# Scores of two heads in 64-row tiles of TensorE, instead of one head doubled over 128 rows

## The chip, the cores and the metric

The kernel runs on one core of a Trainium2 chip. The metric is the device time of one execution in microseconds (us); lower is better. The core has five engines that run side by side and wait for each other by semaphores: TensorE (PE in the profile; its weight loads are PEld), VectorE (DVE), ScalarE (ACT), GpSimd (POOL) and SyncE (SP), which here issues the DMAs.

## What is computed

An attention with a narrow window and block summaries is followed by a mixture of four dense experts, all in float32. The part that the change touches is the scores:

```python
B, H, S, D = 4, 8, 768, 64        # q, k, v; block, window = 32, 16
k_sum = k.reshape(B, H, nb, block, D).max(axis=3)
scores_l = scale * np.matmul(q, k.transpose(0, 1, 3, 2))       # only |i - j| < 16 counts
scores_s = scale * np.einsum('bhsd,bhnd->bhsn', q, k_sum) + np.log(block)
a = softmax(concat(where(mask_l, scores_l, -1e9), scores_s))
x = matmul(a, concat(v, v_sum))                                 # 3072 tokens of 512
# experts: out += p[:, e] * (relu(x @ w1[e]) @ w2[e]),  w1: 512x1024, w2: 1024x512, e = 0..3
```

## The kernel before

**Pieces.** Attention is cut into 64 pieces `n`: batch `b = n // 16`, a block `i` of 96 queries, and a group `g` of four heads. A piece of 96 queries sees 128 keys (its window) and the 24 block maxima of k, so its scores are 96 x 152 for each head. The first 8 pieces run by a path of their own (`first_tokens`, `piece`), with plain float32 products; the other 56 go through `load_piece`, `stage_a`, `scores`, `probs`, `transposed`, `values` and `to_x`.

**A piece before.** `load_piece` (line 519) issues two DMAs: `kr`, 128 partitions x 4 heads x 128 keys from `kD`, which holds k twice (once in partitions 0 to 63, once in 64 to 127), and `qv`, four heads of q (doubled over the partitions in the same way) beside v. `stage_a` (528) copies the block maxima behind the keys on POOL, and splits k into a high part (rounded to the fp32r type, ACT) and a low part (POOL), two heads at a time; q is rounded on ACT, and POOL overwrites partitions 64 to 127 of it by the low part. A head has 64 features, so one matmul with 128 rows multiplies q's high part (rows 0 to 63) and q's low part (rows 64 to 127) with k's high part at once, and a second one with k's low part: two products per head, four heads, eight matmuls `psc` per piece. `scores` (561) is called twice per piece, `half` 0 and 1, with two heads each; each half has one PSUM bank, the tile `psc`. VectorE then reads the bank, adds the mask and finds the maxima (`ms`, `nb`), and ScalarE takes the exponentials. Further on, `values` (625) issues the matmuls `px`: 12 of them per piece (16 in the first batch), each with 64 output columns, two at a time side by side in the array.

**The banks.** PSUM has three pools: `ps_mm` (4 banks), `ps_sc` (2 banks, tag `sc`) and `ps_av` (2 banks). The tag `sc` has a second user: when two token blocks are worked as a pair (`first`, line 1420, and `second_sevens`, 1325), the accumulator with key `a` of each unit, `pha` or `poa` in the profile, also takes an `sc` bank. In `first`, a unit is seven products of six matmuls in the order a, d, b, a, b, c, b; bank `a` is held from the first product until the fourth has been read.

**The experts.** `plan` gives six stages: token block 0 with experts 0 and 1, block 1 with experts 1 and 0, both with experts 2 and 3 (fp32r matmuls `ph`, `po`), then three pairs of token blocks (16-bit float matmuls `pha` to `phd`, `po`, then `poa` to `pod`). Between their units `advance` (1501) calls the attention steps whose key is due: `scores` half 0 at k, half 1 at k + 0.3, `values` at k + 2.0 (k + 1.5 for n below 16), so that the values of piece n and half 0 of piece n + 2 fall on the same place.

**The order.** Nothing is issued where it is called. Each call records a `Step`, and `order_of` (162) puts all of them into one order: it plays the program with its own durations (`PE`, `ACT`, ... from line 109), gives the buffers of a tag to its tiles in the order in which they are first used, and lets TensorE take, of the matmuls whose operands and whose bank are there, the one that comes first in the written order. A tile whose bank is still held isn't there yet, and TensorE goes on with other matmuls. On the chip each engine then follows its list in order and waits where it must.

**Block maxima of k.** `setup_k` (453) loads k by pairs of heads (`kch`), VectorE takes the maxima into `ksr`, and `spread_k` (445) doubles them into `ks` with four small DMAs; for batch 0 `first_tokens` calls `spread_k` (line 965).

Of the kernel before, what the change touches and what calls it, by code (L numbers as in the profile page):

```python
# [10 lines left out]
F32 = mybir.dt.float32  # L11
F32R = mybir.dt.float32r
# [3 lines left out]
ALU = mybir.AluOpType  # L16
AX = mybir.AxisListType

P = 128
B, H, S, D = 4, 8, 768, 64  # L20
E, DM, DF = 4, 512, 1024
BLK, WIN = 32, 16
NB = S // BLK
QB = 96
KW = 128
KA = KW + NB
NQ = S // QB
G = 4
# [5 lines left out]
SCALE = 1.0 / math.sqrt(D)  # L34
# [25 lines left out]
def _win0(i):  # L60
    return min(max(QB * i - WIN, 0), S - KW)
# [7 lines left out]
def columns(ap):  # L69
    return math.prod(n for _, n in ap.ap[1:])  # L70
# [15 lines left out]
class Step:  # L86
# [22 lines left out]
    def PE(self, op, kw):  # L109
        n, w = self.moved(), self.read[0]  # L110
        if op == "transpose":
            return 95.0, 260.0
        if w.dtype == F32:
            return 65.0 + 1.75 * n, 230.0 + 1.75 * n
        if columns(w) == D:
            return 22.0 + 0.18 * n, 215.0 + 0.25 * n
        t = max(70.0, 0.453 * n) + 15.0 * (n < 200) if w.dtype == F32R else max(45.0, 0.4235 * n)
        return t, t + 165.0

    def ACT(self, op, kw):  # L120
# [167 lines left out]
def attn_moe(ctx: ExitStack, tc: tile.TileContext, qvL, qv0, v0L, kD, kT, vT, w1L, w2L, dpL, cst, out):  # L288
# [3 lines left out]
    class Engine:  # L292
# [5 lines left out]
        def __getattr__(self, name):  # L298
# [3 lines left out]
            return issue  # L302

    V, A, PL, PE, SP = (
        Engine(e, k)
        for e, k in ((nc.vector, "DVE"), (nc.scalar, "ACT"), (nc.gpsimd, "POOL"), (nc.tensor, "PE"), (nc.sync, "SP"))
    )
# [12 lines left out]
    def pool(name, bufs=1, **kw):  # L320
        return Pool(name, bufs, **kw)
# [3 lines left out]
    def spare_x(n):  # L325

        return n % 2 == 1 and n < XFREE

    sb = pool("sb")
    ps_mm = pool("ps_mm", 4, space=bass.MemoryType.PSUM)  # L330
    ps_sc = pool("ps_sc", 2, space=bass.MemoryType.PSUM)
# [98 lines left out]
    ksum = {}  # L430
# [5 lines left out]
    def load_chunk(b, hp, ch, src):  # L436
        SP.dma_start(ch, src[b, 2 * hp : 2 * hp + 2].rearrange("h d s -> (h d) s"))

    def block_stats(ch, dst, hp, op):
        V.tensor_reduce(dst[:, hp, :], ch.rearrange("p (n k) -> p n k", k=BLK), axis=AX.X, op=op)  # L440

    def chunk(name):
        return sb.tile([P, S], F32, name=name, tag="chunk", bufs=CHUNKS)

    def spread_k(b, ksr):
        ks = sb.tile([P, H, NB], F32, name=f"ks{b}", tag="ks", bufs=2)
        ks_v = ks.rearrange("p (a j) n -> p j a n", j=2)
        for half in range(2):
            for j in range(2):
                SP.dma_start(ks_v[half * D : (half + 1) * D, j], ksr[j * D : (j + 1) * D])  # L450
        ksum[b] = ks

    def setup_k(b):
        ksr = sb.tile([P, G, NB], F32, name=f"ksr{b}", tag="ksr")
        for hp in range(H // 2):
            ch = chunk(f"kch{b}_{hp}")
            load_chunk(b, hp, ch, kT)
            block_stats(ch, ksr, hp, ALU.max)
        spread_k(b, ksr)

    def setup_v(b):
        vsr = sb.tile([P, G, NB], F32, name=f"vsr{b}", tag="vsr")
# [55 lines left out]

    def load_piece(n):
        b, i, g = n // 16, (n // 2) % NQ, n % 2  # L520
        h0, w0 = g * G, _win0(i)
        kr = sb.tile([P, G, KA], F32, name=f"kr{n}", tag="kr", bufs=2)
        qv = sb.tile([P, G * QB + G * D], F32, name=f"qv{n}", tag="qv", bufs=2)
        SP.dma_start(kr[:, :, 0:KW], kD[b, :, h0 : h0 + G, w0 : w0 + KW])
        SP.dma_start(qv, qvL[b, i, g])
        st[n] = dict(kr=kr, qv=qv)

    def stage_a(n):
        b, i, g = n // 16, (n // 2) % NQ, n % 2
        h0 = g * G  # L530
        t = st[n]
        qr = t["qv"][:, 0 : G * QB].rearrange("p (h s) -> p h s", s=QB)
        vr = t["qv"][:, G * QB :].rearrange("p (h d) -> p h d", d=D)
        kr = t["kr"]
        PL.tensor_copy(kr[:, :, KW:KA], ksum[b][:, h0 : h0 + G, :])
        ks = []
        tag, bufs = ("x", NX) if spare_x(n) else ("kl", 2)
        for half in range(2):
            k2 = sb.tile([P, 2, 2, KA], F32R, name=f"ks{n}_{half}", tag=tag, bufs=bufs)
            hs = slice(2 * half, 2 * half + 2)  # L540
            A.copy(k2[:, :, 0, :], kr[:, hs, :])
            PL.tensor_tensor(k2[:, :, 1, :], kr[:, hs, :], k2[:, :, 0, :].bitcast(F32), op=ALU.subtract)
            ks += [k2[:, 0], k2[:, 1]]
        qs = sb.tile([P, G, QB], F32R, name=f"qs{n}", tag="qs", bufs=1)
        A.copy(qs, qr)
        PL.tensor_tensor(qs[D:P], qr[D:P], qs[D:P].bitcast(F32), op=ALU.subtract)
        v12 = sb.tile([P, G, 2, D], F16 if b else BF16, name=f"v12_{n}", tag="v12", bufs=3)
        if b:
            A.mul(vr, vr, scale_v[b])
            A.copy(v12[:, :, 0, :], vr)  # L550
            PL.tensor_tensor(v12[:, :, 1, :], vr, v12[:, :, 0, :], op=ALU.subtract)
            t.update(ks=ks, qs=qs, v=v12)
            return
        v3 = sb.tile([P, G, D], BF16, name=f"v3_{n}", tag="v3", bufs=3)
        A.copy(v12[:, :, 0, :], vr)
        PL.tensor_tensor(vr, vr, v12[:, :, 0, :], op=ALU.subtract)
        A.copy(v12[:, :, 1, :], vr)
        PL.tensor_tensor(v3, vr, v12[:, :, 1, :], op=ALU.subtract)
        t.update(ks=ks, qs=qs, v=(v12, v3))

    def scores(n, half):
        i = (n // 2) % NQ
        t = st[n]
        mask = masks[0 if i == 0 else (2 if i == NQ - 1 else 1)]
        if half == 0:
            t["ms"] = sb.tile([QB, G, KA], F32, name=f"ms{n}", tag="ms", bufs=2)
            t["nb"] = sb.tile([QB, G], F32, name=f"nb{n}", tag="nb", bufs=2)

            t["rs"] = sb.tile([QB, G, 2], F32, name=f"rs{n}", tag="rs", bufs=3)[:, :, 0]
        ms, nb, rs, qs, ks = (t[w] for w in ("ms", "nb", "rs", "qs", "ks"))  # L570
        heads = (2 * half, 2 * half + 1)

        def maximum(j, o, add):

            V.tensor_tensor_reduce(
                ms[:, j, :], o, add, scale=-SCALE, scalar=3.0e38,
                op0=ALU.add, op1=ALU.min, accum_out=nb[:, j : j + 1],
            )

        psc = ps_sc.tile([P, 2, 256], F32, name=f"psc{n}_{half}", tag="sc")  # L580
        for j in heads:
            o = psc[:QB, j % 2, :KA]
            PE.matmul(o, qs[:, j, :], ks[j][:, 0, :], start=True, stop=False)
            PE.matmul(o, qs[:, j, :], ks[j][:, 1, :], start=False, stop=True)
        for j in heads:
            maximum(j, psc[:QB, j % 2, :KA], mask)
        for j in heads:
            A.activation(
                ms[:, j, :], ms[:, j, :], AF.Exp, bias=nb[:, j : j + 1], scale=-1.0,
                accum_out=rs[:, j : j + 1],  # L590
            )
# [126 lines left out]
    def first_tokens(units):  # L718
        kch = [sb.tile([P, S], F32, name=f"k0{hp}", tag="x", bufs=NX) for hp in range(4)]
        qvs = []  # L720
        for m in range(per):
            tag, bufs = ("w1", NW1) if m < 4 else ("x", NX)
            qvs.append(sb.tile([P, 2 * (QB + 2 * D)], F32, name=f"qv0_{m}", tag=tag, bufs=bufs))
        vch = [sb.tile([P, S], F32, name=f"v01_{c}", tag="x", bufs=NX) for c in range(2)]
        ksr = sb.tile([P, G, NB], F32, name="ksr0", tag="ksr")
        vsr = sb.tile([P, 2, NB], F32, name="vsr0", tag="vsr")
        v0 = sb.tile([NST, 512], F32, name="v0_0", tag="chunk", bufs=CHUNKS)
        vn, vsf = {}, {}
# [94 lines left out]
        def piece(n, m, s):  # L823
# [84 lines left out]
            def x_part(w):  # L908
# [5 lines left out]

            steps = (
                (v_ones,), (scores, 0), (scores, 1), (maxima, 0), (maxima, 1), (exps, 0), (exps, 1),
                (summary,), (turn, 0), (turn, 1), (turn_summary,), (turned,), (turned_summary,),
                (gather,), (divide,), (x_turn,), (x_part, 0), (x_part, 1),
# [25 lines left out]
        for fc in range(EARLY):  # L944
            at(KEYS[4 + fc], split_early, fc, "1", PL)
            at(KEYS[12 + fc], split_early, fc, "2", V)
            at(KEYS[12 + fc] - 1e3, load_early, w2L, fc, "2")
        at(-1.0, load_piece, per)
        at(-1.0, load_piece, per + 1)
        at(99.0, load_early, w1L, 4, "1")  # L950
        at(99.0, load_early, w1L, 5, "1")
# [10 lines left out]
            at(KEYS[8 + fc], next, units)  # L962
        for _, _, f, a in sorted(todo, key=lambda s: s[:2]):
            f(*a)
        spread_k(0, ksr)
        vmean0.append(v0)


# [513 lines left out]
    for n in range(per, NTB * per):  # L1482
        k = n + SHIFT * (n >= 2 * per)
        if n > per + 1:
            steps.append((k - 2.0, load_piece, n))
        steps += [
            (k - 0.6, stage_a, n),
            (k + 0.0, lambda m: scores(m, 0), n),
            (k + 0.3, lambda m: scores(m, 1), n),
            (k + 0.4, probs, n),  # L1490
            (k + 0.8, transposed, n),
            (k + (1.5 if n < 2 * per else 2.0), values, n),
            (k + (1.8 if n < 2 * per else 2.3), to_x, n),
        ]
    for b in range(1, B):
        k = 2 * per * b + SHIFT
# [23 lines left out]
    for (tbs, experts), end in zip(plan, ENDS):  # L1520
        pair = tbs if isinstance(tbs, int) else None
        n = 2 if pair else len(tbs)
# [91 lines left out]
```

## Time and profile before

| what | value |
|---|---|
| median of 3 runs | 1099.01 us (1097.31 to 1099.16) |
| the profiled execution | 1096.94 us |
| span of the profiled execution, first to last instruction | 1095.2 us |
| mean granted TensorE clock | 0.997 |
| VectorE busy | 810.6 us (74%) |
| ScalarE busy | 694.9 us (63%) |
| GpSimd busy | 563.9 us (51%) |
| DMA moved | 184.10 MB, q1 busy 56.5% of 16 engines |

How to read it: busy time is the union of an engine's instructions. Matmuls are pipelined: a matmul is shown from its start to its modelled end, so that the records of neighbours overlap, and the cost of one is read from the distance between starts. In the timeline a row merges instructions of one kind that follow each other: start, time from the first start to the last end, and a count. Almost every instruction is recorded under line 300, the helper that issues it, so groups are told apart by their tiles.

### The profile page before, as it was taken

What the parts mean: (1) busy time and instruction counts of PE and PEld (TensorE: products, weight loads), DVE (VectorE), ACT (ScalarE), POOL (GpSimd) and SP (SyncE); (2) the same over time, 40 slices, a digit from 0 to 9 for tenths busy, and PEclk for the clock granted to TensorE, in tenths of its full rate; (3) what the DMA queues carried; (4) which work ended last, traced back from release to release, by engine and by line L of the source; (5) the groups of instructions that cost most, each with busy time, mean ns of one, the idle gap of its engine ahead of it and who ended that gap; (6) DMA issues with size and microseconds to landing.
All of it is one profiled execution on the core that took longest, in us unless ns stands there. A gap on an engine that the chain in (4) does not pass through costs nothing.

```text
span 1095.2 us, 20517 instructions
## 1 busy us (share of the span) xinstructions
PE 1077.9 (98%) x6994; PEld 747.4 (68%) x6994; DVE 810.6 (74%) x1959; ACT 694.9 (63%) x1882; POOL 563.9 (51%) x650
## 2 busy tenths in 40 slices
PE   8998989999999999999999999999999999999998
PEld 6887879898897655555555565555555468686867
DVE  6789889998988898787776555456546684969473
ACT  5778577774677999987764565556435572848170
POOL 2499757772855989976643222234102251717060
PEclk9999999999999999999999999999999999999999
DMA  7478757776646897787786564474621350515001
GB/s 270 153 220 214 197 156 200 187 192 171 187 132 182 302 257 234 243 259 239 262 266 184 162 177 140 143 206 126 179 71 52 123 173 1 174 48 164 1 16 59
DMA packets 169305, 184.10 MB, mean 168 GB/s; under 512 B 79344, under 2 KB 115184, under 8 KB 169200
## 3 DMA queue, kind: packets, MB, share of 16 engines
q1 hardware_dynamic: 169200, 182.79, 56.5%
q8 instruction: 55, 0.90, 0.3%
q14 instruction: 50, 0.41, 0.1%
HBM read 131.76 MB, written 34.08 MB: 151 GB/s over the span
## 4 chain that ended last, share of the span: by engine, by line
PE 86%; DVE 5%; POOL 3%; ACT 3%; issue 1%; DMA 1%; SPq 0%; POOLq 0%; DVEq 0%; ACTq 0%
PE po L300 30%; PE phb L300 12%; PE ph L300 9%; PE pha L300 8%; PE psc L300 4%; PE pob L300 4%; PE phc L300 4%; PE phd L300 4%; PE poa L300 3%; PE px L300 2%; PE pod L300 1%; PE poc L300 1%; PE pav L300 1%; DVE wmax L300 1%; DVE ms L300 1%
## 5 line engine op out<-in xcount | busy, mean ns | idle before, releaser
L300 PEld LDWEIGHTS <-w1g 128*128 128x128 f16 x2016 | 195.7, 98 | 145.2 <-issue 1.8
L300 PE MATMUL po<-w2s,h 128*128 128x512 f16 x1152 | 279.8, 379 | 0.0
L300 PEld LDWEIGHTS <-h 128*128 128x128 f16 x1584 | 151.7, 98 | 116.4
L300 PE MATMUL phb<-x_t,w1g 128*128 128x384 f16 x864 | 164.1, 326 | 0.6 <-DVE phc L300 0.2
L300 PE MATMUL ph<-xh,w 128*128 128x384 f32 x512 | 139.7, 342 | 4.3 <-ACT w L300 2.4
L300 PE MATMUL po<-w,hh 128*128 128x512 f32 x384 | 124.3, 401 | 0.2 <-DVE hl L300 0.2
L300 POOL TENSOR_TENSOR ks<-kr,ks 128x304 fp32r<-128x304 f32 x112 | 104.6, 938 | 36.4 <-ACT ks L300 33.2
L300 ACT ACTIVATE ms<-ms,nb 96x152 f32<-96x152 f32 x256 | 104.2, 414 | 18.6 <-DVE nb L300 18.2
L300 PE MATMUL pha<-x,w1g 128*128 128x384 f16 x576 | 111.5, 326 | 0.0
L300 DVE CUSTOM_DVE_ANT_0 ms<-psc,c_sb 96x152 f32<-96x152 f32 x256 | 70.6, 306 | 54.7 <-PE psc L300 52.0
L300 POOL TENSOR_TENSOR qs<-qv,qs 64x384 fp32r<-64x384 f32 x56 | 60.0, 1072 | 93.0 <-ACT qs L300 67.2
L300 POOL TENSOR_TENSOR w<-wr,w 128x512 fp32r<-128x512 f32 x60 | 82.5, 1383 | 32.1 <-ACT w L300 19.6
L300 PEld LDWEIGHTS ph<-xh,w 128*128 128x128 f32 x512 | 93.6, 189 | 6.4 <-ACT w L300 2.9
L300 POOL TENSOR_TENSOR v<-qv,v 128x256 f16<-128x256 f32 (+1 forms) x56 | 43.5, 777 | 88.9 <-ACT v L300 69.2
L300 PE MATMUL ph<-xl,w 128*128 128x384 f32 x256 | 86.3, 338 | 0.0
L300 PEld LDWEIGHTS po<-w,hh 128*128 128x128 f32 x384 | 70.8, 190 | 15.1 <-DVE hl L300 0.9
L300 DVE TENSOR_TENSOR aw<-ms,aw 96x512 f16<-96x512 f32 x112 | 73.3, 681 | 8.2 <-ACT aw L300 7.8
L300 POOL TENSOR_TENSOR w2g<-wr,w2g 128x256 f16<-128x256 f32 (+1 forms) x32 | 31.3, 986 | 90.3 <-ACT w2g L300 90.2
L300 PE MATMUL po<-w,hl 128*128 128x512 f32 x192 | 76.2, 399 | 0.0
L300 PE MATMUL psc<-ks,qs 128*96 128x152 f32 x448 | 64.3, 266 | 5.2 <-DVE nb L300 3.5
L300 PEld LDWEIGHTS psc<-ks,qs 128*96 128x96 f32 x448 | 52.9, 166 | 15.5 <-DVE nb L300 4.0
L300 PEld LDWEIGHTS <-hs 128*128 128x128 f16 x576 | 56.3, 98 | 6.6
(184 smaller groups left out, 2214.5 us busy)
## 6 DMA issues: line engine op xcount, KB each, us to landing
wr<-in_w2L SPq DMA_DIRECT2D x104, 256.0 KB, 3.2
qv<-in_qvL SPq DMA_DIRECT2D x56, 320.0 KB, 3.5
kr<-in_kD SPq DMA_DIRECT2D x56, 256.0 KB, 3.5
w1g<-wdg SPq DMA_DIRECT2D x28, 512.0 KB, 3.6
wr<-in_w1L SPq DMA_DIRECT2D x44, 256.0 KB, 3.4
w1g<-wdg SPq DMA_DIRECT2D x28, 384.0 KB, 3.1
wx<-in_w1L SPq DMA_DIRECT2D x32, 256.0 KB, 4.2
wdg<-w1g SPq DMA_DIRECT2D x16, 512.0 KB, 4.4
```

The costliest lines, as they stand in the source:

```text
L300: program.append(Step(self.key, lambda: getattr(self.engine, name)(*a, **kw), name, a, kw))
```

## The change

Two heads now share the partitions: head 2p in rows 0 to 63 and head 2p + 1 in rows 64 to 127, for k, q and the block maxima. Each head has three products of 64 rows (high x high, high x low, low x high), and consecutive matmuls alternate between the two halves of the array and between two PSUM banks, `psc[0]` and `psc[1]`. `scores` is called once per piece, with all four heads. The arrays `kD` and `qvL` are made as before; less of them is loaded. `spread_k` is gone; `ksr` itself is used. In `order_of`'s durations a matmul with 64 rows is put down at half.

```diff
 class Step / def PE:
+        t *= 0.5 if w.ap[0][1] == D else 1.0

-    def spread_k(b, ksr):
-        ks = sb.tile([P, H, NB], F32, name=f"ks{b}", tag="ks", bufs=2)
-        ks_v = ks.rearrange("p (a j) n -> p j a n", j=2)
-        for half in range(2):
-            for j in range(2):
-                SP.dma_start(ks_v[half * D : (half + 1) * D, j], ksr[j * D : (j + 1) * D])
-        ksum[b] = ks
 def setup_k(b):
+        ksr = ksum[b] = sb.tile([P, G, NB], F32, name=f"ksr{b}", tag="ksr", bufs=2)
...
-            load_chunk(b, hp, ch, kT)
+            for j in range(2):
+                r = slice(j * D, (j + 1) * D)
+                SP.dma_start(ch[r], kD[b, r, 2 * hp + j])
...
-        spread_k(b, ksr)

 def load_piece(n):
-        kr = sb.tile([P, G, KA], F32, name=f"kr{n}", tag="kr", bufs=2)
-        qv = sb.tile([P, G * QB + G * D], F32, name=f"qv{n}", tag="qv", bufs=2)
-        SP.dma_start(kr[:, :, 0:KW], kD[b, :, h0 : h0 + G, w0 : w0 + KW])
-        SP.dma_start(qv, qvL[b, i, g])
+        kr = sb.tile([P, 2, KA], F32, name=f"kr{n}", tag="kr", bufs=2)
+        qv = sb.tile([P, 3 * QB + G * D], F32, name=f"qv{n}", tag="qv", bufs=2)
+        heads = kT[b, g * G : (g + 1) * G].rearrange("(h j) d s -> (j d) h s", j=2)
+        SP.dma_start(kr[:, :, 0:KW], heads[:, :, w0 : w0 + KW])
+        for j in range(2):
+            r = slice(j * D, (j + 1) * D)
+            SP.dma_start(qv[r, 0 : 3 * QB], qvL[b, i, g, r, j * QB : (j + 3) * QB])
+        SP.dma_start(qv[:, 3 * QB :], qvL[b, i, g, :, G * QB :])

 def stage_a(n):
-        PL.tensor_copy(kr[:, :, KW:KA], ksum[b][:, h0 : h0 + G, :])
-        for half in range(2):
-            k2 = sb.tile([P, 2, 2, KA], F32R, name=f"ks{n}_{half}", tag=tag, bufs=bufs)
-            hs = slice(2 * half, 2 * half + 2)
-            A.copy(k2[:, :, 0, :], kr[:, hs, :])
-            PL.tensor_tensor(k2[:, :, 1, :], kr[:, hs, :], k2[:, :, 0, :].bitcast(F32), op=ALU.subtract)
-        qs = sb.tile([P, G, QB], F32R, name=f"qs{n}", tag="qs", bufs=1)
-        A.copy(qs, qr)
-        PL.tensor_tensor(qs[D:P], qr[D:P], qs[D:P].bitcast(F32), op=ALU.subtract)
+        PL.tensor_copy(kr[:, :, KW:KA], ksum[b][:, 2 * g : 2 * g + 2, :])
+        ks = sb.tile([P, 2, 2, KA], F32R, name=f"ks{n}", tag=tag, bufs=bufs)
+        A.copy(ks[:, 0], kr)
+        PL.tensor_tensor(ks[:, 1], kr, ks[:, 0].bitcast(F32), op=ALU.subtract)
+        qs = sb.tile([P, 2, 2, QB], F32R, name=f"qs{n}", tag="qs", bufs=1)
+        A.copy(qs[:, 0], qr)
+        PL.tensor_tensor(qs[:, 1], qr, qs[:, 0].bitcast(F32), op=ALU.subtract)

-    def scores(n, half):
+    def scores(n):
...
-        psc = ps_sc.tile([P, 2, 256], F32, name=f"psc{n}_{half}", tag="sc")
-        for j in heads:
-            o = psc[:QB, j % 2, :KA]
-            PE.matmul(o, qs[:, j, :], ks[j][:, 0, :], start=True, stop=False)
-            PE.matmul(o, qs[:, j, :], ks[j][:, 1, :], start=False, stop=True)
+        psc = [ps_sc.tile([P, 2, 256], F32, name=f"psc{n}_{j}", tag="sc") for j in range(2)]
+        for pair in range(2):
+            for m, (x, y) in enumerate(((0, 0), (0, 1), (1, 0))):
+                for j in range(2):
+                    r = slice(j * D, (j + 1) * D)
+                    PE.matmul(
+                        psc[j][:QB, pair, :KA], qs[r, x, pair, :], ks[r, y, pair, :], start=m == 0, stop=m == 2
+                    )
...
-            (k + 0.0, lambda m: scores(m, 0), n),
-            (k + 0.3, lambda m: scores(m, 1), n),
+            (k + 0.0, scores, n),
```

More of the change, by code (lines that the diff above doesn't have):

```diff
@@ L443, in chunk @@
         return sb.tile([P, S], F32, name=name, tag="chunk", bufs=CHUNKS)
-    def spread_k(b, ksr):
-        ks = sb.tile([P, H, NB], F32, name=f"ks{b}", tag="ks", bufs=2)
-        ks_v = ks.rearrange("p (a j) n -> p j a n", j=2)
-        for half in range(2):
-            for j in range(2):
-                SP.dma_start(ks_v[half * D : (half + 1) * D, j], ksr[j * D : (j + 1) * D])
-        ksum[b] = ks
     def setup_k(b):
-        ksr = sb.tile([P, G, NB], F32, name=f"ksr{b}", tag="ksr")
+        ksr = ksum[b] = sb.tile([P, G, NB], F32, name=f"ksr{b}", tag="ksr", bufs=2)
         for hp in range(H // 2):
             ch = chunk(f"kch{b}_{hp}")
-            load_chunk(b, hp, ch, kT)
+            for j in range(2):
+                r = slice(j * D, (j + 1) * D)
+                SP.dma_start(ch[r], kD[b, r, 2 * hp + j])
             block_stats(ch, ksr, hp, ALU.max)
-        spread_k(b, ksr)
     def setup_v(b):
@@ L520, in load_piece @@
         b, i, g = n // 16, (n // 2) % NQ, n % 2
-        h0, w0 = g * G, _win0(i)
-        kr = sb.tile([P, G, KA], F32, name=f"kr{n}", tag="kr", bufs=2)
-        qv = sb.tile([P, G * QB + G * D], F32, name=f"qv{n}", tag="qv", bufs=2)
-        SP.dma_start(kr[:, :, 0:KW], kD[b, :, h0 : h0 + G, w0 : w0 + KW])
-        SP.dma_start(qv, qvL[b, i, g])
+        w0 = _win0(i)
+        kr = sb.tile([P, 2, KA], F32, name=f"kr{n}", tag="kr", bufs=2)
+        qv = sb.tile([P, 3 * QB + G * D], F32, name=f"qv{n}", tag="qv", bufs=2)
@@ L526, in load_piece @@
+        heads = kT[b, g * G : (g + 1) * G].rearrange("(h j) d s -> (j d) h s", j=2)
[4 more added lines that the diff above has]
+        SP.dma_start(qv[:, 3 * QB :], qvL[b, i, g, :, G * QB :])
         st[n] = dict(kr=kr, qv=qv)
     def stage_a(n):
-        b, i, g = n // 16, (n // 2) % NQ, n % 2
-        h0 = g * G
+        b, g = n // 16, n % 2
@@ L531, in stage_a @@
         t = st[n]
-        qr = t["qv"][:, 0 : G * QB].rearrange("p (h s) -> p h s", s=QB)
-        vr = t["qv"][:, G * QB :].rearrange("p (h d) -> p h d", d=D)
+        qr = t["qv"][:, 0 : 3 * QB].rearrange("p (h s) -> p h s", s=QB)[:, 0:3:2, :]
+        vr = t["qv"][:, 3 * QB :].rearrange("p (h d) -> p h d", d=D)
         kr = t["kr"]
-        PL.tensor_copy(kr[:, :, KW:KA], ksum[b][:, h0 : h0 + G, :])
-        ks = []
+        PL.tensor_copy(kr[:, :, KW:KA], ksum[b][:, 2 * g : 2 * g + 2, :])
@@ L537, in stage_a @@
         tag, bufs = ("x", NX) if spare_x(n) else ("kl", 2)
-        for half in range(2):
-            k2 = sb.tile([P, 2, 2, KA], F32R, name=f"ks{n}_{half}", tag=tag, bufs=bufs)
-            hs = slice(2 * half, 2 * half + 2)
-            A.copy(k2[:, :, 0, :], kr[:, hs, :])
-            PL.tensor_tensor(k2[:, :, 1, :], kr[:, hs, :], k2[:, :, 0, :].bitcast(F32), op=ALU.subtract)
-            ks += [k2[:, 0], k2[:, 1]]
-        qs = sb.tile([P, G, QB], F32R, name=f"qs{n}", tag="qs", bufs=1)
-        A.copy(qs, qr)
@@ L564, in scores @@
         mask = masks[0 if i == 0 else (2 if i == NQ - 1 else 1)]
[L565 to L573, printed above, removed]
+        ms = t["ms"] = sb.tile([QB, G, KA], F32, name=f"ms{n}", tag="ms", bufs=2)
+        nb = t["nb"] = sb.tile([QB, G], F32, name=f"nb{n}", tag="nb", bufs=2)
+        rs = t["rs"] = sb.tile([QB, G, 2], F32, name=f"rs{n}", tag="rs", bufs=3)[:, :, 0]
+        qs, ks = t["qs"], t["ks"]
+        psc = [ps_sc.tile([P, 2, 256], F32, name=f"psc{n}_{j}", tag="sc") for j in range(2)]
[6 more added lines that the diff above has]
+                    )
+        for j in range(G):
             V.tensor_tensor_reduce(
-                ms[:, j, :], o, add, scale=-SCALE, scalar=3.0e38,
+                ms[:, j, :], psc[j % 2][:QB, j // 2, :KA], mask, scale=-SCALE, scalar=3.0e38,
                 op0=ALU.add, op1=ALU.min, accum_out=nb[:, j : j + 1],
             )
-        psc = ps_sc.tile([P, 2, 256], F32, name=f"psc{n}_{half}", tag="sc")
-        for j in heads:
-            o = psc[:QB, j % 2, :KA]
-            PE.matmul(o, qs[:, j, :], ks[j][:, 0, :], start=True, stop=False)
-            PE.matmul(o, qs[:, j, :], ks[j][:, 1, :], start=False, stop=True)
-        for j in heads:
-            maximum(j, psc[:QB, j % 2, :KA], mask)
-        for j in heads:
+        for j in range(G):
             A.activation(
@@ L724, in first_tokens @@
         vch = [sb.tile([P, S], F32, name=f"v01_{c}", tag="x", bufs=NX) for c in range(2)]
-        ksr = sb.tile([P, G, NB], F32, name="ksr0", tag="ksr")
+        ksr = ksum[0] = sb.tile([P, G, NB], F32, name="ksr0", tag="ksr", bufs=2)
         vsr = sb.tile([P, 2, NB], F32, name="vsr0", tag="vsr")
@@ L964, in first_tokens @@
             f(*a)
-        spread_k(0, ksr)
         vmean0.append(v0)
```

## The prediction, made before the result was known

> **What bounds the kernel now.** I read the page first, for the share of each engine.
>
> ```profile
> PE 1077.9 (98%) x6994; PEld 747.4 (68%) x6994; DVE 810.6 (74%) x1959; ACT 694.9 (63%) x1882; POOL 563.9 (51%) x650
> ```
>
> TensorE is busy nearly all the time, so a matmul's time counts unless an idle stretch swallows it. Next, the windows by stage (length, then busy time and count of PE, PEld, DVE, ACT, POOL; clock, DMA share, GB/s) and TensorE's waits in the first of these stages (total, times, longest).
>
> ```profile
> 45.00:215.00 170.00, 160.11 (x1007) 138.11 (x1006) 155.26 (x377) 124.58 (x364) 135.48 (x138) 0.98 0.73 196
> 366.00:785.00 419.00, 418.88 (x2613) 233.54 (x2612) 292.62 (x738) 288.54 (x814) 219.61 (x274) 1.00 0.70 212
> ```
>
> ```profile
> PE psc L300 <- DVE nb L300: 3.5, 2, 3.3
> PE ph L300 <- ACT w L300: 2.4, 2, 1.3
> PE ph L300 <- POOL w L300: 1.8, 3, 0.7
> PE psc L300 <- POOL qs L300: 1.6, 2, 0.8
> ```
>
> From 45 to 215 us TensorE idles 170.00 - 160.11 = 9.9 us, of which 5.8 us are put down to ScalarE and GpSimd and 3.5 us to VectorE. In the pair stages (366 to 785 us) it idles 0.1 us of 419: there only the matmuls themselves, in their order, can change the time. How many score matmuls lie in either part, the windows of the tile `psc` show (PE, PEld, DVE):
>
> ```profile
> 53.00:366.00 313.00, 30.50 (x232) 27.63 (x232) 32.23 (x116) 0.99 0.70 188
> 366.00:785.00 419.00, 33.79 (x216) 25.30 (x216) 29.71 (x108) 1.00 0.70 212
> ```
>
> At eight per piece these are 29 pieces before the pair stages and 27 within. The busy times here are no costs, since records overlap; the cost is read from distances between starts. So I took TensorE's timeline around one unit of a pair (start, length, count).
>
> ```profile
> 427.23 1.14 PE L300 MATMUL pha<-x,w1g 128*128 128x384 f16 x6
> 428.30 0.32 PE L300 MATMUL px<-awT,v 128*64 128x192 f16 x4
> ...
> 428.76 0.57 PE L300 MATMUL psc<-ks,qs 128*96 128x152 f32 x4
> 429.17 1.47 PE L300 MATMUL po<-w2s,h 128*128 128x512 f16 x6
> 430.47 1.14 PE L300 MATMUL phd<-x_t,w1g 128*128 128x384 f16 x6
> 431.45 1.46 PE L300 MATMUL po<-w2s,h 128*128 128x512 f16 x6
> 432.74 1.14 PE L300 MATMUL phb<-x_t,w1g 128*128 128x384 f16 x6
> 433.58 0.62 PE L300 MATMUL psc<-ks,qs 128*96 128x152 f32 x4
> 434.05 1.47 PE L300 MATMUL po<-w2s,h 128*128 128x512 f16 x6
> 435.36 1.14 PE L300 MATMUL pha<-x,w1g 128*128 128x384 f16 x6
> ```
>
> Six `phd` take 431.45 - 430.47 = 0.98 us, 0.163 each, or 0.42 ns per column. From the start of `phb` to the `po` behind the scores are 434.05 - 432.74 = 1.31 us; less 0.98, a block of four `psc` costs **0.33**. In the same way `px` and the four `psc` behind it cost 429.17 - 427.23 - 0.98 = **0.96**. A piece before costs 0.96 + 0.33 = 1.29 with its values, where they adjoin. The window also shows where the scores lie: behind the first `pha` (427.23) and before the second (435.36), while that accumulator holds one of the two `sc` banks. Half 0 and half 1 get by with the other bank, one after the other.
>
> **The change: the matmuls.** Six pairs take the place of eight matmuls. First the pace, from these rows (the first: tile `psc`, min/median/max in ns).
>
> ```profile
> L300 PE MATMUL psc<-ks,qs x448: 229/249/439, 53.2 to 781.4; 128*96 128x152 f32 x150
> ```
>
> ```profile
> 306.76 0.49 PE L300 MATMUL psc<-ks,qs 128*96 128x152 f32 x4
> 307.50 0.21 PE L300 MATMUL px<-awT,vs 72*64 72x96 f16 x2
> 307.64 0.44 PE L300 MATMUL ph<-xh,w 128*128 128x384 f32 x1
> 307.92 0.34 PE L300 MATMUL ph<-xl,w 128*128 128x384 f32 x1
> ```
>
> Four `psc` last 0.49 from the first start to the last end and one lasts 0.249, so they start (0.49 - 0.249) / 3 = 0.08 apart. Their 152 columns are worth only 0.06 at 0.42 ns: the load of 96 weight columns sets the pace, and half the rows don't shorten it by themselves. Whether two row tiles load side by side, the first tokens show: their float32 scores already use 64 rows, half 0 in one part of the array and half 1 in the other, and by chance two halves once meet.
>
> ```profile
> 6.76 0.27 PEld L300 LDWEIGHTS psc<-k,qv 64*96 64x96 f32 x4
> 7.17 0.25 PEld L300 LDWEIGHTS psc<-k,qv 64*96 64x96 f32 x2
> ```
>
> Four loads in 0.27 where both halves run, two in 0.25 where one runs: tiles load independently. So a pair costs one slot of 0.08, and six pairs five slots and the last columns, 0.40 + 0.06. The same region has the price of entering 64-row tiles.
>
> ```profile
> 12.49 0.41 PE L300 MATMUL pT<-c_sb,ms 96*128 96x96 f32 x3
> 12.74 0.25 PE L300 MATMUL pT<-c_sb,sm 96*96 96x96 f32 x1
> 12.92 0.46 PE L300 MATMUL psc<-k,qv 64*96 64x128 f32 x2
> ```
>
> Three `pT` take 0.25, 0.08 each, so the last one's columns end at 12.82 and the first 64-row matmul starts at 12.92: 0.10 in which nothing streams, and its load (0.08) hides behind nothing. Leaving a tile shape shows at `px` (64 columns): the last starts at 307.50 with 96 columns (0.04), `ph` at 307.64, so 0.10 again, and that `ph` lasts 0.44 instead of 0.34, its weight load of 0.10 being bare. Before 16-bit weights this is less:
>
> ```profile
> 413.66 0.33 PE L300 MATMUL phd<-x_t,w1g 128*128 128x384 f16 x1
> ...
> 414.38 0.50 PE L300 MATMUL phd<-x_t,w1g 128*128 128x384 f16 x2
> ```
>
> Two `phd` last 0.50, against 0.33 + 0.16, so 0.01; and 12 `px` by themselves cost 414.38 - 413.66 - 0.16 = 0.56. The `psc` before have all 128 rows and neither entry nor exit.
>
> A page of the Trainium skill speaks against this change too: TensorEngine Tiling (Array Packing), Tiling Modes, Key Properties, says that a change of the tiling mode, unlike a change of tile, drains TensorE. The three gaps of 0.10 agree; without it, the sum would be that of the second rival.
>
> A block of 12 alone thus costs 0.10 + 0.08 + 0.40 + 0.06 + 0.10 + 0.01 = 0.75 before 16-bit weights (0.84 before fp32r), against 2 x 0.33 = 0.66 (0.74, two blocks, each with some 0.04 of bare load: an estimate from `ph`'s 0.10 less the 0.06 of columns). Behind `px` the exit of `px` becomes the entry: 0.56 + 0.08 + 0.40 + 0.06 + 0.10 = 1.20 against 1.29. So packed scores gain 0.09 beside `px` and lose 0.09 or 0.10 alone. **The saving of products is paid back in drains.**
>
> **The banks.** This is the larger term. Both tiles of a piece are now wanted at once. While `pha` holds a bank, only `psc[0]` gets one; its six matmuls are ready, and the planner lets TensorE take what is ready. `psc[1]` becomes ready when VectorE has read `psc[0]`, or `pha` has been read, some matmuls later. Then the six of each tile run alone: two blocks of 0.75 each instead of one. The slots do not shrink, since 0.08 is the pace of one tile. In the rows above, half 0 at 428.76 lies so. Going through the pair stages, 18 of 27 pieces start between the first and the second `pha` of a unit: 12 from 371 to 574 us, with only 420 excepted, and 6 of the later ones (624, 645, 673, 686, 738, 751). The last of them:
>
> ```profile
> 747.76 0.81 PE L300 MATMUL pha<-x,w1g 128*128 128x384 f16 x4
> ...
> 751.23 0.57 PE L300 MATMUL psc<-ks,qs 128*96 128x152 f32 x4
> ...
> 755.54 1.15 PE L300 MATMUL pha<-x,w1g 128*128 128x384 f16 x6
> ```
>
> A split piece costs 1.20 + 0.75 - 1.29 = +0.66 beside `px` (15 pieces) and 1.50 - 0.66 = +0.84 alone (542, 558 and 574).
>
> **The other engines.** Per piece one cast and one subtraction of 128x304 go, and those of q become 128x192.
>
> ```profile
> L300 POOL TENSOR_TENSOR ks<-kr,ks 128x304 fp32r<-128x304 f32 x112 | 104.6, 938 | 36.4 <-ACT ks L300 33.2
> L300 POOL TENSOR_TENSOR qs<-qv,qs 64x384 fp32r<-64x384 f32 x56 | 60.0, 1072 | 93.0 <-ACT qs L300 67.2
> ```
>
> GpSimd loses 0.94 + about half of 1.07 + a little for the copy of the maxima, say 1.5 us per piece; ScalarE some 0.6 (one cast, and a third of q's). Before 366 us that can only return idle time of TensorE: at most the 9.9 us. The 5.8 us behind ScalarE and GpSimd are the part to which it applies; VectorE, with 155 of 170 us, keeps all its work and becomes the next to be late. I take half, **-3** us; ends: -9.9, and +3.3, should the longest wait for `nb` come twice now that a piece wants both banks free. After 366 us it is worth nothing.
>
> DMAs: a piece loads 128 KB of k, 2 x 72 KB of q and 128 KB of v instead of these.
>
> ```profile
> qv<-in_qvL SPq DMA_DIRECT2D x56, 320.0 KB, 3.5
> kr<-in_kD SPq DMA_DIRECT2D x56, 256.0 KB, 3.5
> ```
>
> Four issues for two, 400 KB for 576 KB, and `spread_k` with its four small transfers per batch is gone, while `setup_k` issues eight loads instead of four. On SP the new issues stand before the same batch's weights. I cost this at nothing: the loads are due two pieces ahead, behind full TensorE work; were that cover gone, one landing time, 3.5 us, could show once or twice in the early stage, inside the bounds above.
>
> **The sum.** Pair stages: 15 x 0.66 + 3 x 0.84 = 12.4; unsplit 6 x -0.09 + 3 x 0.09 = -0.3. Before them about half of the 29 pieces lie behind `px`: 15 x -0.09 + 14 x 0.10 = 0.0. Together +12.1, less 3: **+9.1 us**. The profiled execution took 1096.94 (span 1095.2); that gives 1106.0. The median of the runs shown is 2.1 higher; I put the forecast halfway, at **1107.0**.
>
> **Rivals.**
> 1. *The split does not happen* (the planner finds both banks, or a wait holds both tiles together). All 27 pieces are packed: 21 x -0.09 + 6 x 0.09 = -1.4 there, 0 before, -3: 1093.5 on the same footing, faster. Against it: half 0 did start with one bank in the rows above.
> 2. *The drain costs nothing and the tiles pack* (the same page, Theoretical Speedup, promises up to 2x for 64 rows; this rival is that promise). Mechanism in this kernel: six slots for eight, 2 x 0.08 x 56 = -9, and -3: 1086, faster. Against it: the three gaps.
> 3. *The two tiles load one after the other where k and q are fp32r.* Six slots more, +0.48 for each of the 38 unsplit pieces: +18, so 1125, slower. Against it: the 0.27 us of four loads; for it: that was plain float32.
> 4. *`psc[1]` waits on the chip* because the planner counts a 64-row matmul at half and so puts it too early behind VectorE: up to two reads of about 0.3, 18 x 0.6 = +11: 1118. It decides if TensorE idles before `psc` in the pair stages.
>
> **Chances.** Forecast 0.62 (its own range 1102 to 1113), rival 1 0.14, rival 2 0.07, rival 3 0.06, rival 4 0.11. Slower by over 0.2% (2.2 us, about what a measurement of this kernel can tell from no change): 0.62 + 0.11 + 0.06, less a little where more idle time returns: 0.75; faster 0.20; within 0.05. The range reaches over rivals 1 and 4 and leaves the other two out: 1090 to 1118.
>
> **What would show it.** In the changed profile about 18 pieces in the pair stages should show two separate blocks of six `psc`, each about 0.75 between its neighbours; a packed block of 12 should take as long as one of six. TensorE's idle time from 45 to 215 us should fall by some 3. If blocks of 12 are the rule in the pair stages, rival 1 is right; if a block of 12 costs about 0.5, rival 2; over 1.1, rival 3. I am wrong altogether if the order around the pairs comes out quite different, since the places of half 0 are taken from the old order.

## The result, and the profile after

The kernel with the change takes **1114.97 us** (median of 4 runs, 1114.76 to 1116.48), beside 1098.16 us for the kernel before in the same runs: a ratio of 1.0157, interval 1.0140 to 1.0175. It is slower, as forecast, but by 17 us where 9 were forecast. The profiled execution took 1114.77 us, 17.8 more than the one before.

The page of the kernel after, in the lines that answer to those of before:

```profile
span 1113.0 us, 20928 instructions
...
PE 1095.3 (98%) x7218; PEld 746.3 (67%) x7218; DVE 792.3 (71%) x1959; ACT 669.9 (60%) x1826; POOL 483.5 (43%) x594
...
L301 POOL TENSOR_TENSOR ks<-kr,ks 128x304 fp32r<-128x304 f32 x56 | 52.3, 933 | 28.5 <-ACT ks L301 26.5
L301 PE MATMUL psc<-ks,qs 64*96 64x152 f32 x672 | 58.3, 258 | 3.7 <-DVE nb L301 2.1
...
L301 POOL TENSOR_TENSOR qs<-qv,qs 128x192 fp32r<-128x192 f32 x56 | 35.0, 626 | 59.5 <-ACT qs L301 47.1
```

What the change takes away is gone: GpSimd has 80 us less to do (563.9 before) and ScalarE 25. VectorE has the same 1959 instructions as before and still 18 us less, as some of them ran shorter; why was not looked into. TensorE is still busy nearly all the time, and it is busy 17 us longer (1077.9 before): 672 matmuls of 64 rows have taken the place of 448 of 128 rows. The windows by stage, columns as before:

```profile
45.00:215.00 170.00, 162.94 (x1084) 136.13 (x1083) 142.72 (x377) 116.82 (x348) 110.39 (x123) 0.99 0.69 175
366.00:785.00 419.00, 415.76 (x2611) 227.21 (x2611) 285.88 (x716) 270.98 (x768) 178.92 (x242) 1.00 0.66 193
```

From 45 to 215 us TensorE now idles 170.00 - 162.94 = 7.1 us instead of 9.9: the relief of the other engines is worth 2.8 us there. In the pair stages it idles 3.2 us where it idled 0.1. How long those stages are is read from the first matmul of `pha`, with which they begin, and the first of `poa`, which comes in their last pair, behind the last piece; what follows it takes as long as before. Tile views of before, then of after (count, min/median/max in ns, first and last start in us):

```profile
L300 PE MATMUL pha<-x,w1g x576: 326/326/339, 366.2 to 1061.0; 128*128 128x384 f16 x192
...
L300 PE MATMUL poa<-w2g,h x288: 272/273/273, 895.5 to 1087.5; 128*128 128x256 f16 x144
```

```profile
L301 PE MATMUL pha<-x,w1g x576: 326/326/337, 366.5 to 1078.6; 128*128 128x384 f16 x192
...
L301 PE MATMUL poa<-w2g,h x288: 272/273/273, 913.2 to 1105.1; 128*128 128x256 f16 x144
```

895.5 - 366.2 = 529.3 us before, 913.2 - 366.5 = 546.7 after (below, this stretch stands for the pair stages): **the pair stages hold 17.4 of the 17.8 us**, though only 27 of the 56 pieces lie there. Up to 366 us the two kernels are level. TensorE's timeline of after at one of these pieces shows the first reason (start, length, count):

```profile
448.01 1.14 PE L301 MATMUL pha<-x,w1g 128*128 128x384 f16 x6
449.07 0.32 PE L301 MATMUL px<-awT,v 128*64 128x192 f16 x4
...
449.54 0.73 PE L301 MATMUL psc<-ks,qs 64*96 64x152 f32 x6
450.20 1.47 PE L301 MATMUL po<-w2s,h 128*128 128x512 f16 x6
451.51 0.49 PE L301 MATMUL phd<-x_t,w1g 128*128 128x384 f16 x2
451.93 0.73 PE L301 MATMUL psc<-ks,qs 64*96 64x152 f32 x6
452.59 0.82 PE L301 MATMUL phd<-x_t,w1g 128*128 128x384 f16 x4
```

The scores stand in two blocks of six, 2.4 us apart, since `pha` took one of the two banks. `px` and the first block cost 450.20 - 448.01 - 0.98 = 1.21 us; the second, in the middle of a `phd` product, costs 452.59 - 451.51 - 2 x 0.163 = 0.75. Six `po` take 451.51 - 450.20, so 0.218 each. With that, a piece whose scores stay together, from the same view later on:

```profile
601.23 1.46 PE L301 MATMUL po<-w2s,h 128*128 128x512 f16 x6
602.62 0.32 PE L301 MATMUL px<-awT,v 128*64 128x192 f16 x4
...
603.08 0.74 PE L301 MATMUL psc<-ks,qs 64*96 64x152 f32 x12
603.75 1.47 PE L301 MATMUL po<-w2s,h 128*128 128x512 f16 x6
```

603.75 - 601.23 - 6 x 0.218 = 1.21: twelve matmuls cost what six cost, so every block that is split off costs 0.75 and saves nothing. The second reason is in four other pieces (in brackets: idle time before, and who ended it):

```profile
617.35 2.11 PE L301 MATMUL po<-w2s,h 128*128 128x512 f16 x9
...
619.85 0.65 PE L301 MATMUL psc<-ks,qs 64*96 64x152 f32 x10
620.91 0.31 PE L301 MATMUL psc<-ks,qs 64*96 64x152 f32 x2 [0.41 <-DVE nb L301]
621.16 1.47 PE L301 MATMUL po<-w2s,h 128*128 128x512 f16 x6
```

Here all twelve are together, but the last two wait for VectorE, and the piece costs 621.16 - 617.35 - 9 x 0.218 = 1.85 us. The first piece of the stages has a wait of its own, inside `phc`:

```profile
370.97 0.73 PE L301 MATMUL psc<-ks,qs 64*96 64x152 f32 x6
...
374.77 0.73 PE L301 MATMUL psc<-ks,qs 64*96 64x152 f32 x6 [1.08 <-DVE h L301]
```

I went through all 27 pieces in this view. Against 1.29 before (0.66 where the scores stood apart from `px`):

| pieces | what they are | cost against before | sum, us |
|---|---|---|---|
| 14 | two blocks of six, one of them behind `px` | 1.21 + 0.75 - 1.29 = +0.67 | +9.4 |
| 4 | two blocks of six, both alone (425, 551, 568, 585 us) | 2 x 0.75 - 0.66 = +0.84 | +3.4 |
| 1 | two blocks and the wait of 1.08 (371 us) | 0.67 + 1.08 | +1.8 |
| 4 | together, last two matmuls wait (619, 672, 714, 741 us) | 1.85 - 1.29 = +0.56 | +2.2 |
| 4 | together, no wait (602, 727, 781, 794 us) | 1.21 - 1.29 = -0.08 | -0.3 |

Together +16.5 of the 17.4 us. (Two of the unsplit pieces, at 602 and 619 us, stood apart from `px` before, where a piece with its values costs 0.56 + 0.66 = 1.22; that makes 0.1 more in all.) TensorE's waits in the pair stages (total, times, longest) name most of the rest:

```profile
PE psc L301 <- DVE nb L301: 1.5, 4, 0.4
PE psc L301 <- DVE h L301: 1.1, 1, 1.1
PE phb L301 <- DVE phc L301: 0.7, 2, 0.5
```

The first two rows are the stops and the wait of 1.08, counted in the table; the third, 0.7 us in which `phb` waits for VectorE to read `phc`, isn't in it. No ScalarE, GpSimd or DMA is among them.

### The profile page after: what moved, and what is told of

Its sections match the earlier page's. It is cut to its first block, busy times and chain, and to the rows that moved or that the text cites. A ratio compares the mean times of both kernels' runs of the same rounds, so it can differ in the third digit from the quotient of the medians.

```text
span 1113.0 us, 20928 instructions
## 1 busy us (share of the span) xinstructions
PE 1095.3 (98%) x7218; PEld 746.3 (67%) x7218; DVE 792.3 (71%) x1959; ACT 669.9 (60%) x1826; POOL 483.5 (43%) x594
## 4 chain that ended last, share of the span: by engine, by line
PE 63%; DVE 1%; ACT 1%; issue 0%; DVEq 0%
PE po L301 23%; PE phb L301 11%; PE pha L301 7%; PE pob L301 4%; PE phc L301 4%; PE phd L301 4%; PE poa L301 3%; PE psc L301 3%; PE poc L301 1%; PE pod L301 1%; PE px L301 1%; DVE s L301 0%; DVE hs L301 0%; ACT hs L301 0%; DVE phc L301 0%
## 5 line engine op out<-in xcount | busy, mean ns | idle before, releaser
L301 PE MATMUL ph<-xh,w 128*128 128x384 f32 x512 | 137.3, 340 | 0.8 <-POOL w L301 0.7
L301 DVE TENSOR_TENSOR aw<-ms,aw 96x512 f16<-96x512 f32 x112 | 65.8, 611 | 10.2 <-ACT aw L301 10.0
L301 POOL TENSOR_TENSOR ks<-kr,ks 128x304 fp32r<-128x304 f32 x56 | 52.3, 933 | 28.5 <-ACT ks L301 26.5
L301 PE MATMUL psc<-ks,qs 64*96 64x152 f32 x672 | 58.3, 258 | 3.7 <-DVE nb L301 2.1
L301 ACT CAST w<-wr 128x512 fp32r<-128x512 f32 x84 | 50.7, 617 | 17.3 <-DMA wr<-in_w1L 5.9
L301 POOL TENSOR_TENSOR qs<-qv,qs 128x192 fp32r<-128x192 f32 x56 | 35.0, 626 | 59.5 <-ACT qs L301 47.1
```

The source lines that it names most:

```text
L301: program.append(Step(self.key, lambda: getattr(self.engine, name)(*a, **kw), name, a, kw))
```

## The experiments

The theory to be tested: the drains around a block and its split over two banks cost the time, not the number of products. The rivals: the planner's halved price of a 64-row matmul misorders the program; the row tiles don't load side by side; the waits between TensorE and VectorE cost more than the blocks.

### Both banks at once

Each matmul is also given the other bank as something it reads, so that the planner can start a block only when it has both.

```diff
                     PE.matmul(psc[j][:QB, pair, :KA], ...)
+                    program[-1].read.append(psc[1 - j][:QB, pair, :KA])
```

> The changed kernel, with each score matmul also counted as a user of the other row tile's bank in the planner, so that a piece's twelve matmuls start only when both banks are there. Bank theory: no block of six is left, every block is twelve at 0.77 to 0.79 us between 16-bit neighbours (1.23 with px before it), the pair stages take about what they took in the kernel before, and the time falls by 16 to 18 us from the changed kernel's 1115, to 1097 to 1099. Rival, the row tiles and their drains by themselves cost the time: packing changes little, at least 1108.

Measured: 1106.91 us beside 1099.84, ratio 1.0070 (1.0054 to 1.0087). All blocks are of twelve and more than half of the loss is gone, but neither theory's number came. The reason shows in TensorE's and in VectorE's timeline of this kernel:

```profile
415.13 0.65 PE L301 MATMUL psc<-ks,qs 64*96 64x152 f32 x10
416.19 0.31 PE L301 MATMUL psc<-ks,qs 64*96 64x152 f32 x2 [0.41 <-DVE nb L301]
```

```profile
415.82 0.31 DVE L301 CUSTOM_DVE_ANT_0 ms<-psc,c_sb 96x152 f32<-96x152 f32 x1 [0.54 <-PE psc L301]
416.06 0.08 DVE L301 DVE_READ_ACCUMULATOR2_ANT nb<- 96x1 f32 x1
416.54 0.31 DVE L301 CUSTOM_DVE_ANT_0 ms<-psc,c_sb 96x152 f32<-96x152 f32 x1 [0.40 <-PE psc L301]
```

A bank holds two heads, one per `pair`. After six matmuls the heads of pair 0 are finished, and VectorE begins to read the first of them when the tenth has ended (415.82). The last two matmuls write the heads of pair 1, another region of the same two banks, and still start only when that read is over. The planner had set this read ahead of the last two matmuls, as it keeps account by regions. The records show what holds them: the weight load ahead of the two matmuls waits for a semaphore, and VectorE's record of `nb` raises it. So the program as built sets this wait. In the pair stages of this kernel eleven blocks stop so: this is the wait that four pieces of the changed kernel show.

### The planner's price

The line that halves the price of a 64-row matmul is taken out; the rest is the changed kernel.

```diff
-        t *= 0.5 if w.ap[0][1] == D else 1.0
```

> The changed kernel without the line that puts a 64-row matmul down at half in the planner. Bank theory: the blocks of six stay (20 pairs of them), time within 3 us of 1115. Rival, the planner's price misplaces the scores: most of the 17 us come back, 1098 to 1105.

Measured: 1115.24 us, ratio 1.0155 (1.0129 to 1.0182), the same as with the line, and the same 19 of the 27 pieces in the pair stages are in two blocks of six. The price isn't the cause of the loss. It does move the waits: the one of 1.08 us is gone, and all eight unsplit pieces now stop for VectorE (3.5 us in nine waits).

### The order of the two tiles

Both banks at once, and all six matmuls of one row tile ahead of all six of the other instead of by turns.

```diff
-        for pair in range(2):
-            for m, (x, y) in enumerate(((0, 0), (0, 1), (1, 0))):
-                for j in range(2):
+        for j in range(2):
+            for pair in range(2):
+                for m, (x, y) in enumerate(((0, 0), (0, 1), (1, 0))):
```

> As the first kernel of this set, but all six products of the lower row tile are issued before the six of the upper one, in one block of twelve. If the array takes matmuls strictly in the order of issue, each block has eleven slots of 0.085 us instead of five and costs 0.5 more: 56 x 0.5 = 28 over the first kernel, about 1126. If it looks ahead for the other row tile (in the first tokens the second half's matmuls started when some four of the first half's were still to come), about half of that: 1108 to 1116. If order doesn't matter at all: equal to the first kernel.

Measured: 1109.31 us, ratio 1.0093 (1.0074 to 1.0113). In TensorE's timeline a block alone:

```profile
420.17 1.46 PE L301 MATMUL po<-w2s,h 128*128 128x512 f16 x6
421.56 0.97 PE L301 MATMUL psc<-ks,qs 64*96 64x152 f32 x12
422.47 1.47 PE L301 MATMUL po<-w2s,h 128*128 128x512 f16 x6
```

422.47 - 420.17 - 6 x 0.218 = 0.99. One tile after the other would be 0.75 + 6 x 0.08 = 1.23, by turns it is 0.75. So the tiles overlap even when they aren't issued by turns. 56 pieces at 0.24 more would be 13 us, but the total is only 2.4 above the first edit's. In this order no block stops for VectorE, which gives back some 7.0 (eleven stops at 0.64, the price shown below); the rest of the difference, 4.0, is not assigned. The total by itself thus tells little; the block does.

### The relief alone

The kernel before, with its eight matmuls and their 128 rows, but with one split of k for both halves, and the low part of q for two heads only. Heads 2 and 3 of a piece use the split keys of heads 0 and 1, so their own scores are left out.

```diff
-        for half in range(2):
-            k2 = sb.tile([P, 2, 2, KA], F32R, name=f"ks{n}_{half}", tag=tag, bufs=bufs)
-            ...
+        k2 = sb.tile([P, 2, 2, KA], F32R, name=f"ks{n}", tag=tag, bufs=bufs)
+        A.copy(k2[:, :, 0, :], kr[:, 0:2, :])
+        PL.tensor_tensor(k2[:, :, 1, :], kr[:, 0:2, :], k2[:, :, 0, :].bitcast(F32), op=ALU.subtract)
+        ks = 2 * [k2[:, 0], k2[:, 1]]
...
-        PL.tensor_tensor(qs[D:P], ...)
+        PL.tensor_tensor(qs[D:P, 0:2], ...)
```

> The kernel before, its matmuls and loads untouched, with one cast and one subtraction of k instead of two (heads 2 and 3 of each piece use the split keys of heads 0 and 1) and with q's low part made for two heads only. This leaves part of the scores out. If the lighter GpSimd and ScalarE return idle time of TensorE in the early stage, as the prediction had it: 3 us less, about 1095, with TensorE idle about 7 instead of 9.9 us between 45 and 215 us. Rival, VectorE is the one that is late there: no change, 1098.

Measured over 11 runs: 1096.90 us, ratio 0.9978 (0.9967 to 0.9988), that is 2.4 us less than before. Its window:

```profile
45.00:215.00 170.00, 163.29 (x1023) 141.22 (x1023) 146.62 (x379) 119.20 (x348) 115.71 (x125) 0.98 0.77 200
```

TensorE idles 6.7 us there instead of 9.9. So less work on ScalarE and GpSimd is worth 2 to 3 us, at the place foreseen.

### Whole blocks

Both banks at once, and VectorE's reads tied to the whole bank, so that the planner sees what the program will wait for.

```diff
             V.tensor_tensor_reduce(ms[:, j, :], psc[j % 2][:QB, j // 2, :KA], mask, ...)
+            program[-1].read.append(psc[j % 2][:QB, 1, :KA])
```

> The first kernel (a piece's matmuls start only with both banks), and in the planner each maximum also waits for the last matmul of its bank. In the first kernel ten blocks of twelve in the pair stages stood still for 0.41 us before their last pair, until VectorE had read a finished head in the same bank. Theory: those ten stops cost 0.64 us each with the second entry and exit; without them 6 us less than the first kernel, about 1100.5, and no gap between two psc in the pair stages. Rival, VectorE is only late and the wait moves elsewhere: no change, 1106 to 1107.

Measured over 12 runs: 1097.87 us beside 1097.84, ratio 0.9993 (0.9982 to 1.0003). **The whole loss is gone**, with the same products and the same tiles. A block of twelve in the middle of a `phc` product, in the timeline of this kernel:

```profile
438.96 0.49 PE L301 MATMUL phc<-x,w1g 128*128 128x384 f16 x2
439.38 0.74 PE L301 MATMUL psc<-ks,qs 64*96 64x152 f32 x12
440.05 0.82 PE L301 MATMUL phc<-x,w1g 128*128 128x384 f16 x4
```

440.05 - 438.96 - 2 x 0.163 = 0.76, beside 0.75 for six. By the first starts of `pha` and `poa` (365.6 and 896.5) the pair stages take 530.9 us, 7.7 less than with the first edit alone (368.1 to 906.7, so 538.6). They are 1.6 longer than before, as much as one wait of `phb` for VectorE at 370 us takes. Eleven stops at 1.85 - 1.21 = 0.64 are 7.0 of it; the 0.41 of idle time is only a part of a stop, as the last two matmuls also start anew.

### The second half of that repair alone

The changed kernel with VectorE's reads tied to the bank, but without the first edit.

```diff
+            program[-1].read.append(psc[j % 2][:QB, 1, :KA])
```

> The changed kernel with only the second repair: each maximum waits in the planner for the last matmul of its bank, and the banks are given as before, so that pieces still split. Theory: the four blocks in the pair stages that stood still for 0.41 us lose that and the second entry, 4 x 0.64 = 2.6 us less than 1115, about 1112.5; the blocks of six stay. Rival, this repair is what helped in the fifth kernel: about 1106 or less.

Measured: 1111.16 us beside 1099.56, ratio 1.0103 (1.0070 to 1.0135). The blocks of six stay, the stops go, and so does the wait of 1.08 us: the pair stages (first starts 365.4 and 908.6) take 543.2 us, 3.5 less than in the changed kernel, where 4 x 0.64 + 1.08 = 3.6 were to be had. Of the other 13.9 us of loss there, the 19 split pieces make 13.4 by the table above (15 x 0.67 + 4 x 0.84).

### Tied to the values

Whole blocks, and the `px` matmuls of piece n also made to follow the scores of piece n + 2, so that both shape changes fall together.

```diff
         t["psc"] = psc[0]
...
                     PE.matmul(pxv[o * D : (o + 1) * D, c, w, :], *operands, ...)
+                    if "psc" in st.get(n + 2, ()):
+                        program[-1].read.append(st[n + 2]["psc"][:QB, 1, :KA])
...
-            (k + (1.5 if n < 2 * per else 2.0), values, n),
+            (k + (1.5 if n < 2 * per else 2.01), values, n),
```

> As the kernel with whole blocks, and from the third batch block on the values of piece n are tied behind the scores of piece n + 2, so that both share one change of tile shape. Theory of the drains: some 13 more pieces have px beside psc, each 0.12 us cheaper (0.57 + 0.79 apart, 1.23 together): 1.5 to 2 us less than with whole blocks, 1098 to 1099, level with the kernel before. Rival, the later values stall the stores of x or the bank of px: slower than with whole blocks.

Measured: **1094.94 us**, ratio 0.9964 (0.9949 to 0.9979): some 4 us faster than the kernel before, and 20 than the changed one. The timeline of this kernel:

```profile
436.02 0.38 PE L301 MATMUL po<-w2s,h 128*128 128x512 f16 x1
436.33 0.74 PE L301 MATMUL psc<-ks,qs 64*96 64x152 f32 x12
437.00 0.32 PE L301 MATMUL px<-awT,v 128*64 128x192 f16 x4
...
437.46 1.25 PE L301 MATMUL po<-w2s,h 128*128 128x512 f16 x5
```

437.46 - 436.02 - 0.218 = 1.22 for all of a piece. The pair stages take 527.4 us (363.7 to 891.1), 1.9 less than before; 27 pieces at 1.22 - 1.29 are -1.9 (one of them still stands apart). This is what the packed products are worth there when nothing is split, stopped or left apart. The other 2 us of the gain lie ahead of these stages: from the first `ph` (37.9) to the first `pha` it takes 325.8 us, 2.7 less than before.

### One product

Whole blocks with only high x high: four matmuls per piece instead of twelve, the two products with a low part left out.

```diff
-            for m, (x, y) in enumerate(((0, 0), (0, 1), (1, 0))):
+            for m, (x, y) in enumerate(((0, 0),)):
...
-                        ..., start=m == 0, stop=m == 2
+                        ..., start=m == 0, stop=True
```

> As the kernel with whole blocks, but with the first of each head's three products alone: four 64-row matmuls per piece instead of twelve. This leaves the low parts of q and k out of the scores. If two tiles load side by side, four slots of 0.085 go per piece: 56 x 0.34 = 19 us less, about 1081, and a block alone keeps 0.43 to 0.45 us, which is entry and exit for the most part. If the loads of the two tiles took turns, eight slots would go: 38 us less.

Measured: 1083.23 us, ratio 0.9866 (0.9849 to 0.9883) to before. The timeline of a block alone:

```profile
427.14 1.46 PE L301 MATMUL po<-w2s,h 128*128 128x512 f16 x6
428.52 0.40 PE L301 MATMUL psc<-ks,qs 64*96 64x152 f32 x4
428.85 1.25 PE L301 MATMUL po<-w2s,h 128*128 128x512 f16 x5
```

428.85 - 427.14 - 6 x 0.218 = 0.40. Eight matmuls less save 0.76 - 0.40 = 0.36, or 0.09 for each pair: one slot, so the tiles do load side by side in fp32r (in turn it would be 0.64 or more). And of the 0.76 us of a full block only 6 x 0.08 is the pace of products; the rest is entry and exit. The total fell by 14.6 us and not by the 56 x 0.36 = 20 that the blocks save: from 45 to 215 us TensorE idles 9.7 us again, 6.7 of them for VectorE and 2.9 for GpSimd.

### The kernel before, with 64 rows

The kernel before, whose eight matmuls read only rows 0 to 63: nothing is packed or moved, and the products with q's low part are left out.

```diff
-            PE.matmul(o, qs[:, j, :], ks[j][:, 0, :], start=True, stop=False)
-            PE.matmul(o, qs[:, j, :], ks[j][:, 1, :], start=False, stop=True)
+            PE.matmul(o, qs[:D, j, :], ks[j][:D, 0, :], start=True, stop=False)
+            PE.matmul(o, qs[:D, j, :], ks[j][:D, 1, :], start=False, stop=True)
```

> The kernel before with nothing changed but that its eight score matmuls per piece use rows 0 to 63 alone. This leaves q's low part out of the scores. Same count, same columns, same banks, same order. Theory of the drains: a block of four alone now enters and leaves a tile shape, 0.10 + 0.08 + 3 x 0.085 + 0.06 + 0.10 + 0.03 = 0.62 instead of 0.34, and beside px 1.06 instead of 0.97; with some 75 blocks alone and 37 beside px that is 75 x 0.28 + 37 x 0.09 = 24 us more, about 1122. Rival, a shape with fewer rows costs nothing by itself: no change, 1098.

Measured: 1117.90 us beside 1099.56, ratio 1.0173 (1.0140 to 1.0205): halving the rows alone makes the kernel 19 us *slower*. Its timeline:

```profile
443.35 1.14 PE L300 MATMUL phb<-x_t,w1g 128*128 128x384 f16 x6
444.42 0.56 PE L300 MATMUL psc<-ks,qs 64*96 64x152 f32 x4
444.91 1.25 PE L300 MATMUL po<-w2s,h 128*128 128x512 f16 x5
```

444.91 - 443.35 - 0.98 = 0.58, where the same four matmuls with 128 rows cost 0.33. This is the price of the change of shape by itself, 0.25 us per block; behind `px`, where the shape changes anyway, `px` and the block cost 1.05 against 0.96 (medians over the traces). In this trace 62 of the 112 blocks stand alone and 33 beside `px`: 62 x 0.25 + 33 x 0.09 = 18.5 of the 19.

## Why the prediction was right, and which term was too small

- **The drains.** Forecast: 0.75 for a block alone, 1.20 behind `px`, and a packed block as long as one of six. Measured: 0.75 and 0.76, and 1.21 for six and for twelve. The 64-row kernel shows the price by itself. The page TensorEngine Tiling (Array Packing) of the Trainium skill (Tiling Modes, Key Properties) says that a change of tiling mode drains TensorE. The trace agrees, with 0.25 us per block of four.
- **The pairs.** Forecast: one slot of 0.08 for a pair. Measured: 0.09, and twelve as long as six. The third rival, loading in turn, falls.
- **The second rival**, no drain, would have been 1086 us. Even without split and stop the kernel is level with the one before, so it falls too.
- **The split.** The mechanism was right: a bank held by `pha` parts the two tiles, and with both banks at once no block is split. All 18 pieces that the forecast named are split, and one more. The one that had been excepted (420 us in the old order, 425 in the new) is split too, and lies alone.
- **The term that was too small is the one for the banks**: +12.1 us forecast for the pair stages, +17.4 measured. The step that failed is that the unsplit pieces would be free of waits. Four of them stop at their last two matmuls (2.2 us, where -0.3 was set down for all unsplit ones), and the first split one waits 1.08 us. The split pieces make 1.0 more (13.4 for 12.4, most of it the one more), and `phb` behind VectorE 0.7. The result, 1114.97, thus lies outside the forecast's own range (1102 to 1113); the stated one, 1090 to 1118, holds it only because it was made to reach over the first and the fourth rival. That part is luck. Both repairs together give the whole loss back, either one only a part; that settles it.
- **The fourth rival**, `psc[1]` waiting on the chip for VectorE, is true in small. In the first split piece `psc[1]` does wait for VectorE, 1.08 us, and without the halved price this wait is gone. The other waits, 1.5 us in the pair stages, are for the last two matmuls of blocks that were not split, and without the halved price they grow to 3.5 and the total stays.
- **The first rival**, no split, was put at 1093.5, on the forecast's footing halfway between profile and median; without split and stop the kernel is level with before. Where nearly all blocks also lie beside `px`, the time comes near that number (1094.94).
- **The relief.** -3 forecast; -2.8 of idle time in this kernel, -2.4 of the total by itself. It doesn't show in the total of the changed kernel, as the first tokens end later in its profile: the first `ph` starts at 39.5 us instead of 37.7. In the eleven profiles of this study that start lies anywhere from 37.1 to 40.7, and at 40.0 in the kernel with the relief alone, whose first tokens are as before; whether the change has a part in it stays open. The DMAs, costed at nothing, end no wait of TensorE in the pair stages, and the kernel with whole blocks, which loads in the same way, is level with before. From 45 to 215 us three waits of `px`, 1.8 us in all, now end with the DMA that brings `awT`, the transposed attention weights; before there were none.
- **The time ahead of the pair stages**: -3 forecast, +0.3 measured. Of the 3.3 us between, 1.8 are the first tokens; from there to the first `pha` the kernel gains 1.5 (328.5 to 327.0 us), so that 1.3 of the relief is taken by something that was put at 0.0. By the distances between starts, the blocks of `psc` and `px` between 40 and 366 us cost 38.9 us before and 39.5 after, their waits taken out: that is 0.6 of it. Where the rest comes from stays open.

So the forecast lacked 8.7 us on the profile's footing (+9.1 for +17.8): 5.3 in the pair stages, most of them waits between a block and VectorE, and 3.3 ahead of them.

## What to carry to other kernels

A visit to another tile shape costs entry and exit, here 0.25 us or more with bare weight loads, whatever is done in it: put as many products as possible into one visit, and put it beside another change of shape that must be made anyway. Row tiles that write two banks stay in one block only where both banks are free at the same moment, so a pool of two from which anything else may take a bank can part them. And a planner must hold the resources of a block together, and must keep account by the same unit by which the program waits.

## What the runs showed that had not been expected

- Row tiles overlap beyond their order of issue. With all of one tile's six matmuls first, the records of single instructions have the second tile's first one (known by its length, 0.31 us, like the first tile's first one) start 0.24 us after the block's first (421.80 and 421.56), ahead of three matmuls of the first tile that were issued before it; the block takes 0.99 us, not 1.23.
- A matmul into one half of a bank waited, in this program, for VectorE's read of the other half: 0.41 us, eleven times in one kernel, and 0.64 us of cost for each. The wait is for a semaphore that the program itself sets; what would happen without it, no run shows.
- Halving the rows of a matmul with 4-byte weights gained no time: its pace was that of the load of 96 weight columns, 0.08 us, against 0.06 for its 152 columns, and the change of shape made eight such matmuls dearer.
